# A half of the scores of A behind each pair of w_in products, from batch 4 on

## The chip, the cores and the metric

The kernel runs on one core of a Trainium2 chip. The metric is the time of one execution on the device in microseconds (us), as the median of several runs; lower is better. The profile is that of one further execution, whose own time is given beside its span, the stretch from its first instruction to its last.

## What is computed

The program is an attention of the Nyström kind followed by a feed-forward layer with SiLU. There are 8 batches of 8 heads with 576 tokens of 64 values. Cut to what matters, the reference is:

```
q_lm, k_lm = means of q and of k over 32 segments of 18 tokens      (landmarks)
A = softmax(q k_lm^T / 8)        Bm = softmax(q_lm k_lm^T / 8)       C = softmax(q_lm k^T / 8)
Z = six steps of Z <- 2 Z - Z Bm Z, from Bm^T over its two norms
attn = A Z C v                   x = attn, heads side by side (4608 tokens x 512)
out = silu(x w_in) w_out         (512 -> 2048 -> 512)
```

## The kernel before

**One batch at a time, two batches interleaved.** The feed-forward part of batch b runs in 16 steps, s = 0 to 15 (the loop at L941 and L957). Steps 0 to 7 treat the first 288 tokens, 8 to 15 the other 288. The first layer isn't a product with x: the kernel forms mb = (Z C v) w_in per head first, and then multiplies it with A^T. In each step `l1_mm` (L790) does four TensorE products of 288 columns into a PSUM tile hps, and `l1_act` (L805) applies SiLU on ScalarE, into gT. The second layer is a queue of output blocks of 128 tokens, 16 products of 512 columns each; `l2_mm(n)` (L818) takes the next n of them, and copies a finished block to ost on ScalarE for its way out. How many are taken in which step is written out by hand in the lists `CNT` and `REST` (L847 to L850). 72 are taken in each batch from the third on.

**Between these steps the attention of batch b+1 is worked off**, in a fixed order: the scores of B and C in step 1 (L1015), exponentials in step 2, the six iterations up to step 8 or so, `z_mm` and `z_out` in step 10 (L1179). Then mb of batch b+1 is made by two calls of `m_pair` (L760), in steps 11 and 13 (`mp`, L949). One call does 16 products of 64x32 tiles of the TensorE array with 512 columns. The first eight fill two single PSUM banks (`mp`, in the pools psa and psn of one buffer each), which VectorE copies out at L776, two casts; the other eight fill a double bank (`mpp`), which ScalarE copies out at L777. `a_back` (L707) is a VectorE transpose of a normalised half of A into AT; there are two, after steps 9 and 14 (L1219).

**And batch b+2 is prepared.** `transpose_qk` (L199) turns its q and k on VectorE, in steps 7, 8, 10 and 12. `landmarks_pool` (L226) sums its landmarks on GpSimd, five additions per call, L232 to L240, in steps 4 and 8; the last one writes lmn. After step 13, `lm_t` (L273) is a VectorE transpose of lmn into lmc. For batches from 4 on (`early`, L259) `a_pair` (L622) then does the scores of A in step 15, behind three products of the second layer (L1191): two calls of `a_scores` (L576), 16 products each of 32x32 tiles with 288 columns, each call into a double bank `sa`; two VectorE transposes of them into xs (L627); and two maxima (L631). In step 0 of the next batch `a_sub` (L634) takes the maxima off on GpSimd, and `a_exp_all` follows in step 2. Batch 3 has its `a_pair` in step 0 of batch 2 (L999).

**Buffers.** All double banks (hps, mpp, sa, the scores of C) come from one ring of two, `ps2` (L83). Whoever takes the next one waits until the last but one has been read. mp's two banks have one buffer each.

**Order.** Each engine works through its instructions in the order in which the program issues them (the schedule is manual, L77). So what stands behind a waiting instruction on the same engine waits too.

Of the kernel before, what the change touches and what calls it, by code (L numbers as in the profile page):

```python
# [11 lines left out]
OP = mybir.AluOpType  # L12
AX = mybir.AxisListType
# [30 lines left out]
def kernel(  # L44
# [9 lines left out]
    nc = tc.nc  # L54
    B, H, S, Dh = q.shape
    L = 32
# [5 lines left out]
    HF = S // 2  # L62
# [61 lines left out]
    for j in (1, 0):  # L124
        nc.sync.dma_start(
            out=raw[j], in_=(q, k)[j][0, 0:4].rearrange("h (l t) d -> (h l) (t d)", t=SEG))
# [120 lines left out]
    class Att:  # L247
# [371 lines left out]
                   .to_broadcast((pr, 8 * n, L)), start=False, stop=True)  # L619


        def a_pair(self):  # L622
            self.a_first()
            for i in range(2):
                self.a_scores(i)
            for i in range(2):
                nc.vector.transpose(  # L627
                    out=self.xs[:, i],
                    in_=self.sa[i][:, :, 0:HF].rearrange("p r (t n) -> p r t n", n=L))
            for i in range(2):  # L630
                nc.vector.tensor_reduce(out=self.nm[:, i], in_=self.xs[:, i], op=OP.max,  # L631
                                        axis=AX.X, negate=True)
# [124 lines left out]

        def m_pair(self, f):  # L760
            self.m_done = f + 2
            if f == 0:
                mb_t[self.b] = attp.tile([128, 2, DFF], BF, tag="mb", name="mb")
            m = [psa1("mp"), psn1("mp")]
            m2 = ps2("mpp")
            for i in range(2):
                for j in range(4):
                    for r in range(2):
                        p = slice(64 * r, 64 * r + 64)
                        mm((m2[:, r, :] if i else m[r])[32 * j:32 * j + 32, :],  # L770
                           self.zwT[p, j, :],
                           w_in_sb[p, j, 512 * (f + i):512 * (f + i) + 512],
                           start=True, stop=True)
            o = mb_t[self.b][:, :, 512 * f:512 * f + 1024]
            for r in range(2):
                nc.vector.tensor_copy(out=o[:, r, 0:512], in_=m[r])  # L776
            nc.scalar.copy(out=o[:, :, 512:1024], in_=m2)  # L777

# [59 lines left out]
    def l2_add(b, *blocks):  # L840
        for i in blocks:
# [4 lines left out]

    CNT = {0: [0, 0, 0, 0, 4, 4, 2, 2, 4, 4, 3, 3, 2, 2, 1, 1],  # L847
           1: [1, 0, 1, 4, 2, 12, 12, 0] + [4] * 8,
           2: [8, 4, 12, 12, 3, 3, 2, 2, 3, 3, 3, 3, 3, 2, 2, 7]}
    REST = [3, 4, 12, 12, 3, 2, 2, 2, 4, 4, 4, 3, 3, 3, 3, 8]  # L850


    ORD = (1, 0, 3, 2)
# [18 lines left out]
    a = Att(0)  # L872
# [67 lines left out]
    ready = None  # L940
    for b in range(B):  # L941
        nxt = b + 1 < B
# [3 lines left out]
        a, ready = ready, None  # L946

        d = (2, 3)[b] if b < 2 else 0
        mp = (11, 13) if d == 0 else (14, 15)  # L949

        def l1(s):
            h[s] = l1_mm(b, s)
# [4 lines left out]
        for s in range(NDC):  # L957
# [78 lines left out]
            elif s == d + 2:  # L1036
                a.a_start()
                a.a_scores(0)
                a.a_scores(1)
                a.c_max(1)  # L1040
                a.a_max(0)
                a.c_exp(0)
                a.c_exp(1)
                a.a_scores(2)
                a.b_norm()
                a.a_max(1)
                a.a_max(2)
                a.a_shift(0)
                a.a_exp(0)

                def rest():
                    for i in (1, 2):
                        a.a_shift(i)
                        a.a_exp(i)
                    a.c_transpose(0)
                    a.b_expand()
                    l2_mm(2)
                    a.f_mm()
                    a.b_scale()

                a0.m_unit(2, nc.vector.tensor_copy, nc.scalar.copy, pair=True, before=rest)
                table(AF.Silu)
                a.f_out()
                a.c_out(0)
                load_v(2)
                a0.a_norm(1)
                a0.a_norm(2)
                l2_mm(cnt[s] - 2)
                l1(s)
            elif b == 0:  # L1070
                r = s - d
                n = cnt[s]
                if r > 3:
                    l1(s)
                if r == 3:
                    load_qk(3, (1,))
                    act(s - 1)

                    def step():
                        a.ns_mm()  # L1080
                        a.ns_step()
                        l1(s)

                    a0.m_unit(3, nc.scalar.copy, nc.scalar.copy, before=step)
                    nc.vector.tensor_tensor(out=parity, in0=mask[:, 0:2, 0],
                                            in1=mask[:, 2:4, 0], op=OP.add)
                elif r == 4:
                    a.ns_mm()
                    a.ns_step()
                    act(s)  # L1090
                    a0.a_transpose(1)
                    a0.a_out(nc.vector.tensor_copy)
                    a.c_transpose(1)
                    a.c_out(1)
                    a.a_norm(0)
                    load_qk(3, (0,))
                elif r == 5:
                    act(s)
                    a.ns_mm()
                    a.ns_step()  # L1100
                    a.w_scale()
                    a.a_norm(1)
                elif r == 6:
                    a.ns_mm()
                    a.ns_step()
                    a.a_norm(2)
                    load_qk(3, (3,))
                elif r == 7:
                    a.ns_mm()
                    a.ns_step()  # L1110
                    load_qk(3, (2,))
                    landmarks_pool(2, 0)
                elif r == 8:
                    a.ns_mm(last=True)
                    a.x_out()
                    act(s)
                    l2_mm(n)
                    n = 0
                    a.a_transpose(0)
                    a.a_out(nc.vector.tensor_copy)  # L1120
                elif r == 9:
                    act(s)
                    transpose_qk(2, ORD[0])
                    l2_mm(n)
                    n = 0
                    a.w_mm()
                    a.w_out()
                elif r == 10:
                    a.z_mm()
                    a.z_out()  # L1130
                    transpose_qk(2, ORD[1])
                elif r == 12:
                    a.a_transpose(1)
                    a.a_out(nc.vector.tensor_copy)
                    transpose_qk(2, ORD[2])
                if s in h:
                    act(s)
                if r in (11, 13):
                    a.m_pair(r - 11)
                l2_mm(n)  # L1140
                if r == 13:
                    transpose_qk(2, ORD[3])
            elif s == d + 3:
                l1(s)
                act(s - 1)
                act(s)
                l2_mm(2)
                a.f_mm()
                a.b_scale()
                a.f_out()  # L1150
                a.w_scale()


                nc.gpsimd.tensor_copy(out=gate, in_=a.wsp[:, 0, :])  # L1154
                l2_mm(cnt[s] - 2)
                a.ns_mm()
            elif s <= d + 8:
                l1(s)
                if s == d + 6:
                    a.w_mm()  # L1160
                a.ns_step()
                act(s)
                if s == d + 4:
                    a.a_sum(0)
                elif s == d + 5:
                    a.a_sum(1)
                elif s == d + 6:
                    a.w_out()
                    a.a_rec(0, 2)
                    a.a_mul(0)  # L1170
                    a.a_mul(1)
                l2_mm(cnt[s])
                a.ns_mm(last=(s == d + 8))
            elif s == d + 9:
                l1(s)
                a.x_out()
                act(s)
                l2_mm(cnt[s])
            elif s == d + 10:  # L1179
                l1(s)  # L1180
                a.z_mm()
                a.z_out()
                act(s)
                l2_mm(cnt[s])
            else:
                l1(s)
                act(s)
                if nxt and s in mp:
                    a.m_pair(2 * mp.index(s))
                n = cnt[s]  # L1190
                if s == 15 and ready and ready.early:  # L1191
                    l2_mm(3)
                    n -= 3
                    ready.a_pair()
                l2_mm(n)
            if b == 0:
                if s == 3:
# [1 line left out]
            elif b + 2 < B:  # L1199
# [16 lines left out]
                if s == 15 and b == 1:  # L1216
                    ready = Att(b + 2)
                    ready.lm_t(0, 2)
            back = (9, 14) if d == 0 else (12, 13)  # L1219
            if nxt and b and s in back:  # L1220
                a.a_back(back.index(s))
            if (b, s) == (0, 3):
# [34 lines left out]
```

## Time and profile before

| | us |
|---|---|
| median of 3 runs (lowest, highest) | 260.09 (259.84, 260.16) |
| the profiled execution | 260.13 |
| its span | 258.4 |
| what lies around the span | 1.7 |
| TensorE matmuls busy | 243.5 |
| ScalarE busy | 169.8 |
| VectorE busy | 163.4 |
| GpSimd busy | 128.2 |

In the profile PE is TensorE's products, PEld its loads of weights, DVE is VectorE, ACT is ScalarE, POOL is GpSimd. In a timeline each line gives the start and the duration in us from the span's start, the engine, the line of the kernel, the operation, what it writes and reads, and how many such are merged; a bracket gives the idle time before it and who ended it. A duration of a matmul reaches past the start of the next one, because they are pipelined: what a product costs is the distance of the starts. Steps are found by their hps lines: step 0 of batch 3 begins at 110.13 us, that of batch 4 at 137.96, and that of batch 5 at 165.78. A few matmul records are missing from the trace, so a count can be one short and a start one product late.

### The profile page before, as it was taken

The page shows a single profiled execution, that of the slowest core. Times are in us where ns is not written, and L with a number is a line of the kernel's source. Part 1 is how long each engine was busy: PE and PEld are TensorE (multiplying, and loading weights), DVE is VectorE, ACT ScalarE, POOL GpSimd, SP SyncE. Part 2 cuts the span into 40 slices and gives each one's busy share as a digit, 9 for nine tenths or more (in the row PEclk, how much of TensorE's full clock was granted, in tenths as well). Part 3 has the DMA queues.
Part 4 walks back from the last instruction along what each step waited for, and adds up shares of the span by engine and source line. Part 5 has one row for each costly group of instructions (what it writes and reads, how often), then busy time and mean ns, then how long its engine had stood idle before and what let it go on. Part 6 is the DMA issues. An engine that isn't in the chain of part 4 may idle for free.

```text
span 258.4 us, 6560 instructions
## 1 busy us (share of the span) xinstructions
PE 243.5 (94%) x2706; PEld 138.7 (54%) x2748; DVE 163.4 (63%) x375; ACT 169.8 (66%) x312; POOL 128.2 (50%) x156
## 2 busy tenths in 40 slices
PE   8979999989998999999999999999999999999994
PEld 2646555455554555556654564556545655556553
DVE  5878977858896859776885688667967545000000
ACT  2378975669746875778576957597669858445511
POOL 7716547713899379935993299319923030100000
PEclk9999999999999999999999999999999999999999
DMA  7999999971389993885289418122621500111122
GB/s 219 202 210 207 206 206 213 223 161 30 114 119 237 193 130 64 123 180 142 49 140 198 116 43 133 43 57 88 121 56 44 136 25 24 54 68 43 42 81 81
DMA packets 30061, 31.15 MB, mean 121 GB/s; under 512 B 10960, under 2 KB 21456, under 8 KB 30032
## 3 DMA queue, kind: packets, MB, share of 16 engines
q0 software_dynamic: 14816, 17.76, 42.0%
q1 hardware_dynamic: 15216, 12.98, 17.9%
q8 instruction: 21, 0.34, 0.5%
q14 instruction: 8, 0.07, 0.1%
HBM read 36.70 MB, written 9.44 MB: 179 GB/s over the span
## 4 chain that ended last, share of the span: by engine, by line
PE 73%; DVE 8%; POOL 7%; issue 4%; ACT 4%; DMA 3%; POOLq 0%; ACTq 0%
PE ops L80 39%; PE hps L80 20%; DMA eCT<-eC 3%; PE idle L80 3%; PE bb L80 2%; PE lmp L80 2%; POOL lma L232 2%; DVE cmx L449 2%; PE sa L80 2%; PE mp L80 2%; PE scp L80 1%; PE wp L80 1%; DVE nm L610 1%; PE mpp L80 1%; POOL xs L636 1%
## 5 line engine op out<-in xcount | busy, mean ns | idle before, releaser
L80 PE MATMUL ops<-w_out_sb,gT 128*128 128x512 bf16 (+1 forms) x554 | 138.6, 373 | 4.3 <-issue 3.6
L810 ACT ACTIVATE gT<-hps 128x576 bf16<-128x576 f32 (+2 forms) x128 | 82.6, 652 | 57.1 <-PE hps L80 54.9
L80 PE MATMUL hps<-AT,mb 128*128 128x288 bf16 (+2 forms) x512 | 83.0, 286 | 1.5 <-DVE xs L627 0.7
L80 PEld LDWEIGHTS <-gT 128*128 128x128 bf16 x592 | 54.2, 98 | 48.5 <-issue 8.8
L80 PEld LDWEIGHTS <-mb 128*128 128x128 bf16 x512 | 48.2, 98 | 27.4 <-issue 1.8
L203 DVE STREAM_TRANSPOSE qkT<-nat 128x576 f32<-128x576 f32 x32 | 39.1, 1243 | 0.2
L836 ACT COPY ost<-ops 128x512 f32<-128x512 f32 (+1 forms) x37 | 21.1, 572 | 14.6 <-PE ops L80 11.5
L232 POOL TENSOR_TENSOR lma<-nat 128x1152 f32<-128x1152 bf16 x11 | 26.2, 2381 | 0.4 <-DMA nat<-in_q_dram 0.3
L408 DVE SCALAR_TENSOR_TENSOR fx<-fx,bb 128x320 bf16<-128x320 bf16 (+1 forms) x39 | 17.9, 458 | 11.3 <-PE bb L80 10.5
L636 POOL TENSOR_TENSOR xs<-xs,nm 128x576 f32<-128x576 f32 x12 | 13.6, 1155 | 19.3 <-DVE nm L631 19.3
L776 DVE CAST mb<-mp 128x512 bf16<-128x512 f32 x28 | 18.0, 685 | 7.2 <-PE mp L80 7.2
L165 ACT ACT_TABLE_LOAD x16 | 20.5, 1283 | 1.1 <-PEq L1241 0.8
L1154 POOL COPY gate<-wsp 128x2 f32<-128x2 f32 x6 | 1.1, 186 | 30.7 <-DVE wsp L493 30.7
L692 POOL TENSOR_TENSOR an<-ex,arec 128x576 bf16<-128x576 bf16 x12 | 13.6, 1159 | 5.3 <-DVE arec L678 5.2
L80 PEld LDWEIGHTS <-fx 128*128 128x128 bf16 (+1 forms) x132 | 8.3, 94 | 12.2 <-DVE fx L408 5.2
L80 PE MATMUL bb<-fx 128*128 128x160 bf16 (+2 forms) x132 | 13.5, 212 | 1.2 <-DVE fx L408 1.1
L777 ACT CAST mb<-mpp 128x1024 bf16<-128x1024 f32 x14 | 14.2, 1012 | 0.0
L627 DVE STREAM_TRANSPOSE xs<-sa 128x576 f32<-128x576 f32 x12 | 8.7, 762 | 7.6 <-PE sa L80 7.6
L449 DVE TENSOR_REDUCE cmx<-scp 128x1 f32<-128x576 f32 x16 | 12.0, 752 | 0.5 <-PE scp L80 0.3
L663 DVE TENSOR_REDUCE arec<-ex 128x18 f32<-128x576 bf16 (+2 forms) x17 | 11.7, 689 | 0.0
L814 POOL COPY gT<-gT 128x1024 bf16<-128x1024 bf16 x4 | 4.1, 1037 | 14.9 <-ACT gT L810 14.9
L237 POOL TENSOR_TENSOR lmc<-lmb,lma 128x384 f32<-128x384 f32 x11 | 11.0, 1004 | 0.9
(120 smaller groups left out, 267.7 us busy)
## 6 DMA issues: line engine op xcount, KB each, us to landing
out_dram<-ost SPq DMA_DIRECT2D x35, 256.0 KB, 2.3
v<-in_v_dram POOLq DMA_DIRECT2D x8, 576.0 KB, 7.2
nat<-in_k_dram POOLq DMA_DIRECT2D x15, 288.0 KB, 7.8
nat<-in_q_dram POOLq DMA_DIRECT2D x15, 288.0 KB, 8.3
w_in_sb<-in_moe_w_in_dram POOLq DMA_DIRECT2D x4, 512.0 KB, 14.5
w_out_sb<-in_moe_w_out_dram POOLq DMA_DIRECT2D x4, 512.0 KB, 13.6
raw<-in_k_dram SPq DMA_DIRECT2D x1, 576.0 KB, 4.2
raw<-in_q_dram SPq DMA_DIRECT2D x1, 576.0 KB, 5.1
```

The source lines that it names most:

```text
L80: nc.tensor.matmul(out=o, lhsT=lhsT, rhs=rhs, start=start, stop=stop, skip_group_check=True)
L165: nc.scalar.activation(out=spare[:, 1:2], in_=spare[:, 0:1], func=func)
L203: nc.vector.transpose(out=o.rearrange("p (l t) -> p t l", t=SEG), in_=nat_t[b][:, j, :].bitcast(FP).rearrange("p (t l) -> p t l", l=L))
L232: nc.gpsimd.tensor_tensor(out=a1, in0=nat[:, :, 0:3 * w], in1=nat[:, :, 3 * w:6 * w], op=OP.add)
L408: nc.vector.scalar_tensor_tensor(out=n, in0=self.fx, scalar=2.0, in1=self.p, op0=OP.mult, op1=OP.add if self.tiled else OP.subtract)
L449: nc.vector.tensor_reduce(out=mx, in_=self.s[g][:, :, 0:HF], op=OP.max, axis=AX.XY, negate=True)
L636: nc.gpsimd.tensor_tensor(out=self.xs[:, i], in0=self.xs[:, i], in1=self.nm[:, i].unsqueeze(3).to_broadcast((128, 2, SEG // 2, L)), op=OP.add)
L692: nc.gpsimd.tensor_tensor(out=self.an[:, i].rearrange("p r t l -> p (r t) l"), in0=x, in1=r.unsqueeze(2).to_broadcast((128, SEG, L)), op=O ...
L776: nc.vector.tensor_copy(out=o[:, r, 0:512], in_=m[r])
L777: nc.scalar.copy(out=o[:, :, 512:1024], in_=m2)
L810: nc.scalar.activation(out=gT_t[b][:, 2 * s:2 * s + 2, o + c0:o + c1], in_=h[:, :, 0:c1 - c0], func=AF.Silu)
L836: nc.scalar.copy(out=ost[:, 0:hi - lo], in_=st["ps"][:, 0:hi - lo])
```

## The change

From batch 4 on the scores of A are no longer made together in step 15. Where two more batches follow (b = 2 to 5, the name `both`), the two calls of `m_pair` for batch b+1 move from steps 11 and 13 to steps 14 and 15, each behind two products of the second layer. Each takes along half i = 0 or 1 of the scores of A of batch b+2 (`a_half`), issued directly behind the pair's 16 products. On VectorE the order is then: first cast of the pair, transpose of the half (`a_turn`), second cast, maximum of the half (`a_top`). On ScalarE it is the pair's double bank as before. The numbers of second-layer products are shifted between steps 10 and 15; their sum stays 72. Batch 6 keeps the old list and the old places of the pairs, and the second `a_back` stands after step 13 in place of 14, behind `lm_t` in the batches that have one.

```diff
+        def a_half(self, i):
+            if i == 0:
+                self.a_first()
+            self.a_scores(i)
+        def a_turn(self, i):
+            nc.vector.transpose(out=self.xs[:, i], in_=self.sa[i]...)
+        def a_top(self, i):
+            nc.vector.tensor_reduce(out=self.nm[:, i], in_=self.xs[:, i], op=OP.max, ...)
-        def m_pair(self, f):
+        def m_pair(self, f, other=None):
...
             o = mb_t[self.b][:, :, 512 * f:512 * f + 1024]
+            if other:
+                other.a_half(f // 2)
+            nc.scalar.copy(out=o[:, :, 512:1024], in_=m2)
             for r in range(2):
                 nc.vector.tensor_copy(out=o[:, r, 0:512], in_=m[r])
-            nc.scalar.copy(out=o[:, :, 512:1024], in_=m2)
+                if other:
+                    (other.a_top if r else other.a_turn)(f // 2)
...
-           2: [8, 4, 12, 12, 3, 3, 2, 2, 3, 3, 3, 3, 3, 2, 2, 7]}
-    REST = [3, 4, 12, 12, 3, 2, 2, 2, 4, 4, 4, 3, 3, 3, 3, 8]
+           2: [8, 4, 12, 12, 3, 3, 2, 2, 3, 3, 3, 2, 2, 2, 6, 5],
+           6: [3, 4, 12, 12, 3, 2, 2, 2, 4, 4, 4, 3, 3, 3, 3, 8]}
+    REST = [3, 4, 12, 12, 3, 2, 2, 2, 4, 4, 3, 3, 3, 2, 7, 6]
...
-        mp = (11, 13) if d == 0 else (14, 15)
+        both = b > 1 and b + 2 < B
+        mp = (14, 15) if both or d else (11, 13)
...
-                if nxt and s in mp:
+                n = cnt[s]
+                if both and s in mp:
+                    l2_mm(2)
+                    n -= 2
+                    a.m_pair(2 * mp.index(s), ready)
+                elif nxt and s in mp:
                     a.m_pair(2 * mp.index(s))
-                n = cnt[s]
-                if s == 15 and ready and ready.early:
-                    l2_mm(3)
-                    n -= 3
-                    ready.a_pair()
                 l2_mm(n)
...
-            back = (9, 14) if d == 0 else (12, 13)
+            back = (9, 13) if d == 0 else (12, 13)
```

More of the change, by code (lines that the diff above doesn't have):

```diff
@@ L619, in a_shift @@
                    .to_broadcast((pr, 8 * n, L)), start=False, stop=True)
+        def a_half(self, i):
[3 more added lines that the diff above has]
+        def a_turn(self, i):
+            nc.vector.transpose(
+                out=self.xs[:, i],
+                in_=self.sa[i][:, :, 0:HF].rearrange("p r (t n) -> p r t n", n=L))
+        def a_top(self, i):
+            nc.vector.tensor_reduce(out=self.nm[:, i], in_=self.xs[:, i], op=OP.max,
+                                    axis=AX.X, negate=True)
         def a_pair(self):
```

## The prediction

> **What bounds the kernel now.** I read the page's shares first, then what TensorE waited for, then the timeline of one steady batch. The page and TensorE's waits say (microseconds in total, times, longest):
>
> ```profile
> PE 243.5 (94%) x2706; PEld 138.7 (54%) x2748; DVE 163.4 (63%) x375; ACT 169.8 (66%) x312; POOL 128.2 (50%) x156
> ```
> ```profile
> PE ops L80 <- issue: 3.6, 23, 0.2
> ...
> PE hps L80 <- DVE xs L627: 0.7, 1, 0.7
> ```
>
> TensorE is the bound, at full granted clock in all 40 slices. Hardly any of its waits is for another engine: the one of 0.7 stands at the start of batch 2, for batch 3's scores, which the change leaves alone. What repeats is "issue", 23 times up to 0.2: a bubble around blocks that use the array in small tiles. The stretch that the change touches, on PE, in batch 4 (step 11 is the line at 156.95, step 0 of batch 5 that at 165.78):
>
> ```profile
> 156.95 0.65 PE L80 MATMUL hps<-AT,mb 128*128 128x288 bf16 x4
> 157.53 0.41 PE L80 MATMUL mp<-w_in_sb,zwT 64*32 64x512 bf16 x8
> 157.75 0.40 PE L80 MATMUL mpp<-w_in_sb,zwT 64*32 64x512 bf16 x8
> 158.31 0.59 PE L80 MATMUL ops<-w_out_sb,gT 128*128 128x512 bf16 x2 [0.16 <-issue]
> 158.75 0.65 PE L80 MATMUL hps<-AT,mb 128*128 128x288 bf16 x4
> ...
> 161.68 0.65 PE L80 MATMUL hps<-AT,mb 128*128 128x288 bf16 x4
> 162.17 0.81 PE L80 MATMUL ops<-w_out_sb,gT 128*128 128x512 bf16 x3
> 162.82 0.65 PE L80 MATMUL hps<-AT,mb 128*128 128x288 bf16 x4
> ...
> 164.05 0.70 PE L80 MATMUL sa<-qkT,lmc 32*32 32x288 bf16 x32
> 164.91 1.03 PE L80 MATMUL ops<-w_out_sb,gT 128*128 128x512 bf16 x4 [0.16 <-issue]
> 165.78 0.65 PE L80 MATMUL hps<-AT,mb 128*128 128x288 bf16 x4
> ```
>
> Prices from the starts: a first-layer group 0.49 (161.68 to 162.17), a second-layer product 0.217 (three to 162.82), so 0.92 for a step with two and 1.14 with three. Entering a block of small tiles 0.09 (156.95 + 0.49 to 157.53). Half a pair 0.22. Leaving it 0.13: from 157.75 to 158.75 is 1.00, less 0.22 and three products of 0.65. The scores: 164.05 to 165.78 is 1.73, less 0.13 and five products of 1.08, so 0.26 a half. From 156.95 to 165.78 these prices add up to 8.85 of 8.83. No hidden wait is there to be won; only the bubbles are, 0.22 for each of three blocks a batch.
>
> **The change, part by part.** *The bubbles.* Two blocks instead of three save one entry and one exit, 0.22 a batch, in four batches 0.88. But each new block changes from 64x32 to 32x32 tiles inside. No row has this change. Its ends are 0 (no bubble) and 0.22 (as much as leaving and entering). The nearest row is the product wp, in tiles of 96x32. These are PE's weight loads; first batch 0, where 32x32 tiles follow, then batch 4, where the whole array follows:
>
> ```profile
> 17.75 0.45 PEld L80 LDWEIGHTS <-eCT 96*32 96x32 bf16 x48 [0.23 <-issue]
> 18.23 0.12 PEld L80 LDWEIGHTS <-fx 32*32 32x32 bf16 x8
> ```
> ```profile
> 150.65 0.44 PEld L80 LDWEIGHTS <-eCT 96*32 96x32 bf16 x48 [0.24 <-issue]
> 151.13 0.11 PEld L80 LDWEIGHTS <-gT 128*128 128x128 bf16 x2
> ```
>
> Both take 0.48 to the next load. So leaving small tiles for other small tiles costs as much as leaving them for the whole array, and I take 0.13. Two of them against 0.22 saved is +0.04 a batch: nothing is won.
>
> The Trainium skill speaks against the saving too: TensorEngine Tiling (Array Packing), section Tiling Modes, says that a change of the tiling mode, not of the tile alone, drains the array. By it the number of drains stays six a batch, and the bubbles come to the same sum; if it did not hold between small tiles, the total below would be smaller by about 0.2.
>
> *A new wait: the landmarks.* The scores moved from late in step 15 into step 14, and all the pair work that lay before them moved behind. They need lmc, which needs lmn, which GpSimd finishes at a time of its own. How fast the chain lmn, lm_t, scores can be is seen where PE waited for it, at the start of batch 2; below it is the end of the same GpSimd chain in batches 2 and 4:
>
> ```profile
> 81.59 0.45 POOL L240 TENSOR_TENSOR lmn<-lmd,lmc 128x128 bf16<-128x128 f32 x1
> ...
> 82.08 0.31 DVE L274 STREAM_TRANSPOSE lmc<-lmn 128x128 f32<-128x128 f32 x1 [0.97 <-POOL lmn L240]
> 82.44 0.38 PEld L80 LDWEIGHTS <-lmc 32*32 32x32 bf16 x32 [0.85 <-DVE lmc L274]
> ```
> ```profile
> 105.97 0.46 POOL L240 TENSOR_TENSOR lmn<-lmd,lmc 128x128 bf16<-128x128 f32 x1
> ```
> ```profile
> 160.74 0.46 POOL L240 TENSOR_TENSOR lmn<-lmd,lmc 128x128 bf16<-128x128 f32 x1
> ```
>
> From lmn's end (82.04) to the scores' load is 0.40. GpSimd works without a gap from step 3's gate (146.79 in batch 4) to 161.20, and the change touches nothing up to there, so lmn stays at 161.20 in batch 4 and 106.43 in batch 2 on before's axis; the scores can begin at 161.60 and 106.83.
>
> When does PE get there? *Batch 4:* step 11 starts one product earlier, at 156.73. Steps 11 and 12 (three products, 1.14 each) and 13 (two, 0.92) give step 14 at 159.93; its group and two products 160.85; entry, pair, mode change: 160.94, 161.38, 161.51. It waits 0.09. *Batch 2:* step 11 at 101.93, three steps of 0.92, step 14 at 104.69, the pair's end at 106.14, ready at 106.27. It waits 0.56. Batches 3 and 5 have batch 4's distances (lmn 4.24 and 4.21 behind step 11, against 4.25).
>
> *VectorE behind lm_t.* It waits for lmn in order, and the second a_back, both casts, transpose and maximum queue behind it. Starts follow one another by 0.22 after lm_t (162.15 to 162.37 in batch 4), about 0.68 after a_back (0.74 long), 0.61 after a cast (two take 1.29, one 0.68), 0.69 after a transpose. Batch 4: lm_t 161.24 (0.04 behind lmn, as at 82.08), a_back 161.46, first cast 162.14, transpose 162.75, second cast 163.44 to 164.12. Who waits: the next pair's second bank, from 164.17 (0.05 as from lm_t's end, 82.39, to the load). PE: scores 161.60 to 161.86, exit and five products to 163.07, step 15's group and two products 163.99, entry 164.08. It waits 0.09. Batch 2, with four products: second cast 108.67 to 109.35, PE there at 109.10, wait 0.30.
>
> *ScalarE.* Step 0's hps needs the double bank of the second pair, whose copy on ACT starts 0.48 after mpp (157.75 to 158.23) and takes 1.01. Batch 4: pair 164.17, mpp 164.39, copied and signalled at 165.93. PE: 164.17 + 0.44 + 0.13 + 0.26 + 0.13 + four products 0.87 = 166.00. No wait. Batch 2 with three products: 111.01 against 109.62 + 0.48 + 1.01 + 0.05 = 111.16, wait 0.15.
>
> *Sum.* Step 0 begins at 166.00 instead of 165.78, +0.22 (0.09 + 0.09 + 0.04), three times 0.66; batch 2 gives 111.16 instead of 110.13, +1.03. Together +1.69. The profiled execution took 260.13 (258.4 of span and 1.7 around it), 0.04 above the median: **261.8**.
>
> *At nothing.* The shifted counts keep their sum; in a step with two products SiLU (0.65) still ends before its bank is needed, 1.34 against 1.84 after its group; uncovered, it would cost 0.2 a step. Batch 7's tail has no wait that these counts set. Step 1's group needs the second transpose: 166.0 against 167.1. a_sub gets its second maximum at about 167.3, as before; exp_all is 4 us later. Scores' banks: SiLU of step 14 is done at 161.3. The loads that GpSimd issues in step 14, and SP's, keep their order.
>
> **The rivals.**
> *Nothing measurable (259.6 to 260.6).* The waits are absorbed: lm_t's answer comes 0.1 sooner in batches 3 to 5, and batch 2's wait is partly caught up. For it: three of the four batches sit within 0.1 us of no wait. Against it: batch 2's 0.56 is far above the 0.04 by which lmn's distance differs from batch to batch. With batch 2 at +0.5 and the rest at 0 it gives 260.6.
> *Faster.* The change inside a block costs nothing and no landmarks are awaited: 0.88 less, 259.3. For it, only that no row shows 64x32 to 32x32; against it wp's rows and lmn's.
> *Slower by more: VectorE as the bound.* Place: the chain lm_t to second cast in front of the second pair. If PSUM casts and transposes run slower beside GpSimd, or lmn moves by 0.3, batches 3 to 5 also pay as batch 2 does, about 0.5 to 0.7 each: 1.03 + 1.5 to 2.1, 262.7 to 263.3. It decides from 0.1 us of delay, since there is no slack. Against it: lmb's durations are 0.99 to 1.01 in every place.
>
> **How the numbers follow.** Forecast 0.63 (260.7 to 262.4), slower by more 0.16, nothing measurable 0.14, faster 0.07. About 0.2%, 0.5 us, is what a measurement can tell from no change. The range 260.3 to 263.0 takes in the forecast, most of the upper rival and the near part of the middle one. Faster 0.07, same 0.14, slower 0.79.
>
> **What would show it.** In the changed trace: PE sa waiting for DVE lmc once in each of batches 2 to 5, longest (0.5 or so) in batch 2; mp waiting for the cast; hps for mpp's copy in batch 2; 0.1 or so between mpp's end and sa's first load. Step 0 to step 0 should be 28.0 instead of 27.82 in batches 3 to 5. If sa follows mpp without a gap, or starts before lmn's end + 0.4 on this axis, the prediction is wrong.

## The result, and the profile after

| | before | changed |
|---|---|---|
| median, us | 260.16 (259.84 to 260.32, 5 runs) | 261.37 (261.21 to 261.60, 5 runs) |
| ratio to before, 95% interval | | 1.0048 (1.0033 to 1.0063) |
| profiled execution, span | 260.13, 258.4 | 261.37, 259.6 |

The change makes the kernel 1.2 us slower. The forecast was 261.8, in a range of 260.3 to 263.0. First TensorE's own waits in the changed kernel (microseconds in total, times, longest):

```profile
PE sa L80 <- DVE lmc L274: 0.9, 2, 0.6
PE bb L80 <- DVE fx L408: 0.7, 2, 0.4
PE hps L80 <- ACT mb L771: 0.4, 2, 0.2
PE lmp L80 <- ACT gT L829: 0.4, 1, 0.4
PE hps L80 <- DVE xs L642: 0.3, 1, 0.3
```

The scores wait for the landmarks twice. One of the two, 0.35, is that of batch 3's scores at the start of batch 2, which stood there before. The other, of 0.58, is new. The line "PE ops <- issue" with its 23 bubbles is missing here; that is no gain. This trace kept all 592 second-layer products, where before's kept 554, and before's first product after a block was often the missing one, so that it showed idle time. So that line was no measure of the bubbles around the blocks, as the prediction read it; what a bubble costs (0.09 to 0.13) shows only from start to start.

Where the wait stands is seen in PE's timeline of batch 2. Step 11 begins at 102.00, step 14 at 104.77, step 15 at 108.23, step 0 of batch 3 at 111.22:

```profile
104.77 0.65 PE L80 MATMUL hps<-AT,mb 128*128 128x288 bf16 x4
105.25 0.59 PE L80 MATMUL ops<-w_out_sb,gT 128*128 128x512 bf16 x2
105.78 0.41 PE L80 MATMUL mp<-w_in_sb,zwT 64*32 64x512 bf16 x8
106.01 0.40 PE L80 MATMUL mpp<-w_in_sb,zwT 64*32 64x512 bf16 x8
106.98 0.45 PE L80 MATMUL sa<-qkT,lmc 32*32 32x288 bf16 x16 [0.58 <-DVE lmc L274]
107.36 1.04 PE L80 MATMUL ops<-w_out_sb,gT 128*128 128x512 bf16 x4
108.23 0.65 PE L80 MATMUL hps<-AT,mb 128*128 128x288 bf16 x4
108.72 0.59 PE L80 MATMUL ops<-w_out_sb,gT 128*128 128x512 bf16 x2
109.25 0.64 PE L80 MATMUL mp<-w_in_sb,zwT 64*32 64x512 bf16 x8
109.50 0.60 PE L80 MATMUL mpp<-w_in_sb,zwT 64*32 64x512 bf16 x8
110.03 0.45 PE L80 MATMUL sa<-qkT,lmc 32*32 32x288 bf16 x16
110.41 0.82 PE L80 MATMUL ops<-w_out_sb,gT 128*128 128x512 bf16 x3
111.22 0.65 PE L80 MATMUL hps<-AT,mb 128*128 128x288 bf16 x4
```

From step 11 to step 0 it takes 9.22, against 8.20 before: 1.02 more, nearly the whole loss. The second pair's eight first products are merged to 0.64 instead of 0.41; they wait in their midst for the cast. In front of the last line 0.16 is idle (110.41 and three products of 0.217 give 111.06), for ScalarE's copy. The cause of the 0.58 is GpSimd's last landmark addition, and VectorE's transpose right behind it:

```profile
106.13 0.45 POOL L240 TENSOR_TENSOR lmn<-lmd,lmc 128x128 bf16<-128x128 f32 x1
```
```profile
106.61 0.31 DVE L274 STREAM_TRANSPOSE lmc<-lmn 128x128 f32<-128x128 f32 x1 [2.25 <-POOL lmn L240]
106.85 0.73 DVE L723 STREAM_TRANSPOSE AT<-an 128x576 bf16<-128x576 bf16 x1
107.51 0.65 DVE L794 CAST mb<-mp 128x512 bf16<-128x512 f32 x1
108.09 0.76 DVE L628 STREAM_TRANSPOSE xs<-sa 128x576 f32<-128x576 f32 x1
108.77 0.65 DVE L794 CAST mb<-mp 128x512 bf16<-128x512 f32 x1
```
```profile
110.16 1.01 ACT L792 CAST mb<-mpp 128x1024 bf16<-128x1024 f32 x1 [0.59 <-PE mpp L80]
```

VectorE stood idle for 2.25 us before its transpose, and then all its work of steps 13 to 15 queued up. Its second cast ends at 109.42, after the second pair has begun (109.25); ScalarE's copy of that pair ends at 111.17, just before step 0 (111.22).

The bracket's 0.58 counts from the end that the profile gives to the product before. From start to start, mpp to the scores takes 0.97, where it takes 0.33 without a wait (e5_both, below): 0.64 is lost there. The second pair takes 0.78 from its first product to its scores instead of 0.55, so 0.23. With the 0.16 at step 0 that is 1.03, the whole of the 1.02. In batch 4 the same block has no named wait:

```profile
162.10 0.41 PE L80 MATMUL mp<-w_in_sb,zwT 64*32 64x512 bf16 x8
162.33 0.40 PE L80 MATMUL mpp<-w_in_sb,zwT 64*32 64x512 bf16 x8
162.69 0.45 PE L80 MATMUL sa<-qkT,lmc 32*32 32x288 bf16 x16
163.07 1.25 PE L80 MATMUL ops<-w_out_sb,gT 128*128 128x512 bf16 x5
```

Step 0 to step 0 in batches 3, 4 and 5 is 27.89, 27.88 and 27.86, against 27.83, 27.82 and 27.81: 0.06, 0.06 and 0.05 more, where the prediction had 0.22 each.

### The profile page after: what moved, and what is told of

It reads as the page before. It is cut to its first block, busy times and chain, and to the rows that moved or that the text cites. A ratio compares the mean times of both kernels' runs of the same rounds, so it can differ in the third digit from the quotient of the medians.

```text
span 259.6 us, 6602 instructions
## 1 busy us (share of the span) xinstructions
PE 250.0 (96%) x2748; PEld 138.9 (54%) x2748; DVE 162.4 (63%) x375; ACT 170.5 (66%) x312; POOL 128.0 (49%) x156
## 4 chain that ended last, share of the span: by engine, by line
PE 69%; POOL 13%; DVE 9%; issue 5%; ACT 2%; POOLq 0%; ACTq 0%; DVEq 0%
PE ops L80 37%; PE hps L80 18%; POOL lma L232 4%; PE idle L80 3%; PE lmp L80 2%; PE bb L80 2%; PE sa L80 2%; POOL xs L651 2%; POOL lmc L237 2%; POOL lmb L235 2%; PE mp L80 2%; POOL an L707 1%; DVE xs L642 1%; DVE cmx L449 1%; PE scp L80 1%
## 5 line engine op out<-in xcount | busy, mean ns | idle before, releaser
L80 PE MATMUL ops<-w_out_sb,gT 128*128 128x512 bf16 (+1 forms) x592 | 147.3, 374 | 0.0
L203 DVE STREAM_TRANSPOSE qkT<-nat 128x576 f32<-128x576 f32 x32 | 38.5, 1239 | 0.2
L80 PE MATMUL idle<-zero 128*128 128x512 bf16 x27 | 10.3, 506 | 1.3 <-DVE zero L130 1.3
L235 POOL TENSOR_TENSOR lmb<-lma 128x384 f32<-128x384 f32 x11 | 11.0, 998 | 0.9
```

The source lines that it names most:

```text
L80: nc.tensor.matmul(out=o, lhsT=lhsT, rhs=rhs, start=start, stop=stop, skip_group_check=True)
L203: nc.vector.transpose(out=o.rearrange("p (l t) -> p t l", t=SEG), in_=nat_t[b][:, j, :].bitcast(FP).rearrange("p (t l) -> p t l", l=L))
L235: nc.gpsimd.tensor_tensor(out=a2, in0=a1[:, :, 0:w], in1=a1[:, :, w:2 * w], op=OP.add)
```

## The experiments

The theory: batch 2 loses 1.0 us behind the landmark chain (lmn, lm_t, then VectorE's queue and ScalarE's copy up to step 0), and joining blocks of small tiles neither costs nor saves. The main rival: the split and moved blocks cost about 0.3 us in each of four batches. The last two columns come from the profiled executions.

| kernel | median | ratio to before, 95% interval | batch 2, step 11 to step 0 | batches 3 to 5, step 0 to step 0 |
|---|---|---|---|---|
| before | 260.16 | | 8.20 | 27.83, 27.82, 27.81 |
| changed | 261.37 | 1.0048 (1.0033, 1.0063) | 9.22 | 27.89, 27.88, 27.86 |
| e1_from3 | 260.44 | 1.0003 (0.9991, 1.0015) | 8.20 | 27.93, 27.91, 27.89 |
| e2_fill | 261.62 | 1.0047 (1.0032, 1.0063) | 9.25 | 27.92, 27.91, 27.89 |
| e3_back | 261.37 | 1.0037 (1.0023, 1.0051) | 8.90 | 27.92, 27.93, 27.89 |
| e4_landmarks | 260.42 | 0.9999 (0.9986, 1.0011) | 8.40 | 27.83, 27.84, 27.83 |
| e5_both | 260.46 | 1.0012 (1.0001, 1.0022) | 8.37 | 27.83, 27.83, 27.84 |
| e5_again | 260.41 | 1.0000 (0.9986, 1.0014) | 8.37 | 27.83, 27.84, 27.83 |
| e8_tail | 260.55 | 1.0004 (0.9995, 1.0014) | 8.45 | 27.84, 27.83, 27.83 |
| e6_apart | 261.19 | 1.0035 (1.0022, 1.0047) | 8.55 | 28.05, 28.05, 28.05 |
| e7_top | 264.73 | 1.0172 (1.0152, 1.0192) | 9.92 | 28.70, 28.71, 28.69 |

Each ratio is to runs of before on the same chip (medians 260.30 to 260.35 there for the kernels from e1 on); kernels are compared by these.

**Batch 2 as before** (e1_from3).

```diff
-        both = b > 1 and b + 2 < B
+        both = b > 2 and b + 2 < B
```

with batch 2's old counts, places and `a_pair` in step 15.

> Batch 2 as before, the change in batches 3 to 5 only. Theory (the loss is batch 2's waits behind the landmarks, 1.02 of the 1.2 us; the joined blocks cost and save nothing): 1.0 less than the changed kernel, 260.2 to 260.5, no different from before; step 0 to step 0 in batch 2 is 29.1 to 29.4 again. Rival (the blocks of small tiles, split and moved, cost about 0.3 us in each of the four batches): 261.0 to 261.2.

260.44, and batch 2 is at 8.20 again (29.05 from step 0 to step 0, just under the 29.1 to 29.4 expected). The loss is batch 2's. The same change in three batches costs at most 0.1 each; the rival falls.

**Products moved forward, to cover the wait** (e2_fill).

```diff
-           2: [8, 4, 12, 12, 3, 3, 2, 2, 3, 3, 3, 2, 2, 2, 6, 5],
+           2: [8, 4, 12, 12, 3, 3, 2, 2, 3, 3, 3, 3, 3, 3, 4, 4],
```

> Batch 2's second-layer products moved forward: 3, 3, 3, 4, 4 in steps 11 to 15 instead of 2, 2, 2, 6, 5, so that PE reaches the scores 0.65 us later and no longer waits for the landmarks there. Theory (the chain lmn, lm_t, a_back, cast, transpose, cast, second pair, ScalarE's copy, step 0 sets the end whatever PE does in between): no gain, 261.3 to 261.5, the 0.58 turns up again as longer waits at the second pair and at step 0. Rival (it is the wait at the scores that costs): 0.55 less, 260.8.

No gain: 9.25, and a ratio of 1.0047 against 1.0048; the median of 261.62 is a little above what was expected, on a chip where before took 0.2 longer too. The wait at the scores is gone from the trace, and this is what PE waits for between 101 and 112 us instead; below it the timeline around the second pair:

```profile
PE hps L80 <- ACT mb L792: 0.4, 2, 0.2
```
```profile
108.28 0.65 PE L80 MATMUL hps<-AT,mb 128*128 128x288 bf16 x4 [0.20 <-ACT mb L792]
...
109.29 0.71 PE L80 MATMUL mp<-w_in_sb,zwT 64*32 64x512 bf16 x8
```

Steps 15 and 0 each wait 0.2 for ScalarE's copy by the bracket (0.38 from start to start), and the pair waits longer in its midst (0.30 instead of 0.23). Counted from lm_t (106.73 here, 106.61 in the changed kernel) the scores (107.09, 106.98), the second pair's mpp (109.62, 109.50) and step 0 (111.34, 111.22) stand where they stood. The first wait of such a chain can be filled; the chain's end doesn't move.

**a_back ahead of lm_t** (e3_back).

```diff
                 if s == 13 and b > 1:
+                    a.a_back(1)
                     ready = Att(b + 2)
                     ready.lm_t(0, 2)
...
-            if nxt and b and s in back:
+            if nxt and b and s in back and not (both and s == 13):
                 a.a_back(back.index(s))
```

> The second a_back issued ahead of lm_t in batches 2 to 5, so that it runs on VectorE while that waits for lmn. Theory (VectorE's chain behind lm_t): 0.66 less in the chain; batch 2 keeps the 0.58 at the scores and loses its waits at the second pair and at step 0, 0.3 to 0.45 less, 260.9 to 261.1. Rival (bubbles): 261.4, unchanged.

8.90, 0.32 less than changed, at the lower end of what was expected. The median of 261.37 is above the 260.9 to 261.1 expected. In the runs it is 1.0037 against 1.0048; the intervals overlap, so this step rests on the trace. The pair is whole again (0.41), which is 0.23 of the 0.32. The scores still wait 0.47 instead of 0.58, but that is no effect of the edit: lmn began 4.02 behind step 11 in this trace and 4.13 in the changed kernel's. The wait at step 0 was expected to go and stayed: step 0 comes 1.53 behind mpp (109.47 to 111.00), where PE's own work takes 1.37.

**The landmarks earlier** (e4_landmarks).

```diff
-                if s == 7 + d // 2:
+                if s == (9 if b > 1 else 7 + d // 2):
                     load_v(b + 2)
```

> GpSimd issues the load of v in batches 2 to 5 behind the second landmark sums instead of ahead of them, so lmn ends 0.85 us sooner. Theory (the landmark chain): the wait at the scores in batch 2 goes, and its step 0 comes 0.8 sooner: 260.4 to 260.7. Rival (bubbles): 261.4, unchanged.

GpSimd's issue of the load (0.85) now stands behind the sums, so that lmn is done (105.53) when PE begins the first pair of batch 2 (105.56), and the scores follow that pair without a wait:

```profile
105.08 0.45 POOL L240 TENSOR_TENSOR lmn<-lmd,lmc 128x128 bf16<-128x128 f32 x1
```
```profile
105.79 0.40 PE L80 MATMUL mpp<-w_in_sb,zwT 64*32 64x512 bf16 x8
106.11 0.45 PE L80 MATMUL sa<-qkT,lmc 32*32 32x288 bf16 x16
```

Batch 2 takes 8.40, the three others 27.83 to 27.84, and the ratio is 0.9999. Nothing else of the change was touched, so the loss was the landmarks' lateness. The rest of 0.2 in batch 2 is nearly all ScalarE's copy: mpp at 108.61, and step 0 at 110.18, 1.57 later, where the prediction had 0.48 + 1.01 + 0.05 = 1.54.

**Both cures** (e5_both, and once more as e5_again).

> Both: a_back ahead of lm_t, and the load of v behind the landmark sums. Theory: no wait of TensorE for the landmarks or for VectorE's casts is left in steps 14 and 15, and the time is that of before, 260.1 to 260.4; step 0 to step 0 is 27.8 in batches 3 to 5. If the joining itself saved something, it would show here as a time below before: 259.3 if a change between 64x32 and 32x32 tiles cost nothing. Rival (split blocks cost 0.3 each): 261.1 to 261.4.

> The kernel with both cures once more, beside the one above on the same chip. Theory: with the landmarks earlier, where a_back stands no longer matters, so it takes the same time as the kernel with the load of v moved alone, 260.2 to 260.5 against before's 260.1 to 260.4. Rival (the 0.3 us by which it stood above before is real): 0.3 above the other kernel of this call.

27.83 and 27.84 in batches 3 to 5, the same as before, with no wait left there: the joining itself is worth nothing. (In batch 2 the 0.17 for ScalarE's copy is left, 8.37.) The first median, 260.46, is just above the 260.1 to 260.4 expected. The ratio is 1.0012 in the first set of runs and 1.0000 in the second, so the 0.3 us of the first isn't shown to be the kernel's. With lmn early the place of a_back hardly matters (8.37 against 8.40).

**One product more behind the second pair** (e8_tail): e4_landmarks with 5 and 6 products in steps 14 and 15 of batch 2 instead of 6 and 5.

> The load of v behind the landmark sums, and in batch 2 one product moved from step 14 to step 15 (5 and 6 instead of 6 and 5), to cover ScalarE's copy of the second pair. Theory: the last wait of batch 2 (0.15 to 0.2 at step 0 for that copy) goes as well, nothing is left of the loss and nothing is won: 0.1 to 0.2 below the kernel with the load alone, within 0.15% of before; step 11 to step 0 of batch 2 is 8.20 to 8.25. Rival (joining does save something that a wait has hidden so far): 0.4 or more below before.

A miss: 8.45 instead of 8.20 to 8.25. The same copy has a twin. With three products left behind the first pair, step 15 waited for that pair's copy: mpp ran at 106.31, and step 15 began at 107.84, 1.53 later.

```profile
106.31 0.40 PE L80 MATMUL mpp<-w_in_sb,zwT 64*32 64x512 bf16 x8
...
107.84 0.65 PE L80 MATMUL hps<-AT,mb 128*128 128x288 bf16 x4
```

From mpp PE has 0.22 + 0.11 + 0.26 + 0.13 = 0.72 of its own work, so four products are needed to fill 1.53, behind each pair; batch 2 had seven for both. That is 0.16 of the 0.25 above 8.20. The other 0.09 is the second pair's, which waits in its midst again (mpp at 109.08, scores at 109.50).

**Two products between pair and scores** (e6_apart): both cures, and

```diff
             if other:
+                l2_mm(2)
                 other.a_half(f // 2)
```

with two fewer behind it. ScalarE's copy of the pair's double bank is also issued ahead of these two products, so that it doesn't queue behind a copy of an output block.

> As the kernel with both cures, but two of the second-layer products that stand behind the half of the scores stand between the pair and the half, eight times in all. Theory (a change between small tiles costs 0.11, a way out and in again 0.22): 0.11 more eight times, 0.9 above the kernel with both cures, 261.1 to 261.3. Rival A (nothing is lost between small tiles, so apart costs 0.22 each): 1.8 above, 262.0. Rival B (a change of mode costs the same as the way out and in): no difference.

28.05 against 27.83: 0.22 a batch, 0.11 for each half, as the theory said; by the runs 1.0035 against 1.0012 (0.7 us by the medians), by the spans 1.0 us. PE in batch 4 of it:

```profile
161.97 0.40 PE L80 MATMUL mpp<-w_in_sb,zwT 64*32 64x512 bf16 x8
162.31 0.61 PE L80 MATMUL ops<-w_out_sb,gT 128*128 128x512 bf16 x2
162.84 0.45 PE L80 MATMUL sa<-qkT,lmc 32*32 32x288 bf16 x16
163.22 0.82 PE L80 MATMUL ops<-w_out_sb,gT 128*128 128x512 bf16 x2
```

And the same stretch with both cures and nothing between (e5_both):

```profile
161.46 0.40 PE L80 MATMUL mpp<-w_in_sb,zwT 64*32 64x512 bf16 x8
161.79 0.45 PE L80 MATMUL sa<-qkT,lmc 32*32 32x288 bf16 x16
```

From mpp to the whole array 0.34, and to the scores 0.33: less the 0.22 of the products, 0.12 and 0.11. So from 64x32 tiles a change of shape costs the same to the whole array as to 32x32 tiles. The way back in, after two products (0.43), is 0.53 - 0.43 = 0.10.

**The maximum ahead of the second cast** (e7_top).

```diff
-                if other:
-                    (other.a_top if r else other.a_turn)(f // 2)
+                if other and r == 0:
+                    other.a_turn(f // 2)
+                    other.a_top(f // 2)
```

> The changed kernel with VectorE's order cast, transpose, maximum, second cast: the maximum ahead of the second cast. Theory (the second pair's second bank waits for that cast, and VectorE has no slack before it): the cast ends 0.57 to 0.65 later, and TensorE waits that much longer in each of four batches, 2.3 to 2.6 more, 263.6 to 264.0. Rival (VectorE's order is off the path): 261.4.

The wait came where it was expected, and larger; 264.73 is above the 263.6 to 264.0 expected. PE in batch 2:

```profile
109.33 0.39 PE L80 MATMUL mp<-w_in_sb,zwT 64*32 64x512 bf16 x1
110.37 0.41 PE L80 MATMUL mp<-w_in_sb,zwT 64*32 64x512 bf16 x7 [0.65 <-DVE mb L794]
```

The pair's first product runs, the second one waits for the bank of the second cast. Batches 3 to 5 take 0.82 more each than changed instead of 0.57 to 0.65, and batch 2 takes 0.70 more: 3.2 us in all. VectorE's lines show why:

```profile
108.17 0.76 DVE L628 STREAM_TRANSPOSE xs<-sa 128x576 f32<-128x576 f32 x1
108.97 0.75 DVE L633 TENSOR_REDUCE nm<-xs 128x18 f32<-128x576 f32 x1
109.64 0.68 DVE L794 CAST mb<-mp 128x512 bf16<-128x512 f32 x1
```

The maximum starts 0.80 after the transpose whose result it reads, where in the changed kernel a cast, which reads something else, starts 0.68 after one (108.09 to 108.77 us). So the cast comes 0.80 + 0.67 - 0.68 = 0.79 later.

## Why the prediction was right

- **What bounds.** Right: PE, with no wait to be won. With the waits cured the three steady batches take 27.83 to 27.84, before's time.
- **The bubbles.** Taken as 0.13 for the change inside a block, from wp's rows; measured 0.11 (mpp to sa without a wait). Two such changes against one entry and one exit: 0.22 against 0.22. e6_apart shows that the joining is real, 0.11 cheaper a half than being apart; what it saves goes into splitting the scores in two.
- The Trainium skill (TensorEngine Tiling (Array Packing), section Tiling Modes) says that a change of the tiling mode drains the array; the runs fit this, with 0.11 from 64x32 to 32x32 tiles in e5_both, though none shows the drain itself.
- **Batch 2.** Predicted waits 0.56, 0.30 and 0.15, and +1.03; measured from start to start 0.64 at the scores, a pair 0.23 longer, 0.16 at step 0, and +1.02. The mechanism is right: e4_landmarks shows the cause, e2_fill that it is a chain. That the total agrees to 0.01 is partly luck. lmn ended 4.58 behind step 11 instead of 4.50, which made the first wait longer, and the casts took 0.58 from start to start instead of 0.61, which made the second shorter. In the six traces that keep the load of v ahead of the sums, lmn begins 4.01 to 4.16 behind step 11, so 0.1 either way was open.
- **Batches 3 to 5: the mis-sized term.** +0.22 each was predicted as 0.09 at the scores, 0.09 at the second pair and 0.04 for the bubbles; measured +0.05 to +0.06. In batch 4 the scores' first load follows lmn (161.83 + 0.45 = 162.28) by 0.41, as predicted, but GpSimd's chain from the gate (147.95) took 14.33 instead of 14.41, and the boundary of 0.11 brought PE to the scores at 162.66: a wait of 0.03. The second cast ended at 165.13 and the pair entered at 165.17, since a cast takes 0.57 there and not 0.61: no wait. The bubbles' 0.04 is nothing either (e5_both takes before's 27.83). Of the +0.06 this leaves 0.03 unexplained. In e1_from3 and e2_fill, with the same code in these batches, the scores wait 0.05 to 0.08 and a batch takes 0.08 to 0.10 more; the second pair waits at most 0.01 in either. So the scores' 0.09 was the upper end, and the pair's 0.09 was never there. Both waits hung on differences of 0.1 between chains of 5 to 14 us; the rival of nothing measurable had named that. Three batches at 0.16 less account for the 0.4 us between 261.8 and 261.37. Of the signs that the prediction listed, those of batch 2 came; the named waits of the scores in batches 3 to 5 and the 28.0 us from step 0 to step 0 did not come.
- **At nothing.** a_sub, exp_all and the last batches show nothing: from step 0 of batch 6 to the span's end it is 64.75 against 64.81.

## What to carry to other kernels

When work is moved on a bounding engine, look up when its inputs are ready on the other engines' own time, not only that they were ready where it stood; and follow what queues behind the instruction that waits for them. A wait inside a chain isn't cured by work put in front of it: the chain's start has to move, as one GpSimd instruction's place did here. Count changes of tile shape, not blocks: joining two shapes saves something only if the count goes down.

## What the runs showed of the hardware

A change of tile shape on TensorE costs 0.09 to 0.13 us, in, out or between two small shapes (0.11 from 64x32 to 32x32). A VectorE maximum that reads what the instruction before it wrote starts some 0.12 us later than one that doesn't: 0.80 behind a 128x576 transpose in e7_top, against 0.68 for the cast in the changed kernel. Before, the first maximum, which read the last transpose but one, stood 0.66 behind the last (165.28 to 165.94 in batch 4). That it is the dependence is the likeliest reading; no run isolates it.
